# Six weight groups beside the attention instead of seven, conversions in three stages, and work on x spread out

## The chip, the cores and the metric

The kernel runs on one core of a Trainium2 chip. The metric is device time in microseconds (us) of one execution; times of several executions are given as a median. The core has a matrix engine (TensorE; PE in the profile, PEld for its weight loads), VectorE (DVE), ScalarE (ACT), GpSimd (POOL) and SyncE (SP), which here issues every DMA. Each engine takes its own instructions in order: an instruction that waits for a semaphore holds up what is queued behind it on that engine.

## The reference

```python
# q, k, v: 8 x 12 heads x 448 x 64, float32
scores = q @ k.T / sqrt(64) - log(448)
attn_out = sigmoid(scores) @ v
x = attn_out as 3584 tokens x 768
# w_gate, w_val: 768 x 1536; w_out: 1536 x 768; float64
y = (sigmoid(x @ w_gate) * (x @ w_val)) @ w_out
```

q, k and w_gate are scaled by factors, so values are large; the weights arrive as float64 and are converted on the chip.

## The kernel before

**Stages.** First comes the attention: 24 blocks `m`, of seven beats `g` each (168 beats). A beat issues the score matmuls of one piece (L465), its sigmoid on ScalarE (L473), and the value matmuls of the piece two beats back (L490). Twice a block the two halves of a finished output are added: ScalarE copies one from PSUM (L500), VectorE adds the other (L507), and x goes to DRAM. The two PSUM accumulators of a half are used again some four beats later.

Then come the first two layers in eight visits, numbered 0 to 7. Tokens are taken in four pairs of batch entries; a visit takes one pair and one of two parts of the feed-forward width: visits 0 to 3 have the first part and 56 products each (visit 0 has 53, as visits overlap a little), visits 4 to 6 have 28, visit 7 has 31. A product is nine matmuls of 128x128 by 128x448 (L620); a "tick" is one product. Seven products in place of eight make one two-by-two block product (Strassen's scheme in Winograd's form), so the operands are sums and differences of quarters of x and of quarters of a weight block; n counts the seven. Every operand is a pair of float16 tensors, high part and rest. Two units of seven products are woven into each other two ticks apart, so a product that goes on in the accumulator of another comes four ticks after it, and what reads or copies that accumulator in between (ScalarE's copy at L636, VectorE's add at L603) has three products of time. The output layer (C visits) follows with 21 x 18 matmuls for each pair.

**Conversion of weights.** A weight group is one (jp, t): two 128-column blocks of w_gate (t = 0) or w_val (t = 1), or two 128-row blocks of w_out; twelve groups of the first kind (numbered 0 to 11), six of the second. A group is four tiles of 128x384 float64. For a tile, `Words.first` makes the magnitude (L202 on VectorE in the attention, L205 on ScalarE later), clamps it on GpSimd (L186) and starts the mantissa on VectorE (L187); `Words.second` is four VectorE operations (L196 to L199), the first of which needs the clamp. `convert` is a generator; each `next` is a step. A tile takes two steps, so a group eight; then come the scale (row maxima or sums of absolutes, their broadcast by a small matmul, powers of two) and the seven operands: three quarters cast as they are, four sums made by GpSimd (L247) and cast in the same step; a step later VectorE makes the rest (L217), a step later SyncE stores. Casts are on GpSimd in the attention (L346), on ScalarE later (L343). `todo` holds work for later steps, `now` counts them.

**What sets the order.** The order is written out by hand. In the attention, `FIRST` = 7 groups are spread over `BESIDE` = 160 beats, 72 steps. In the first layers, `due` says how many steps each tick takes: 23 steps (group 7) in ticks 2 to 30 of visit 0, and 91 steps in 188 "calm" ticks: ticks 2 to 29 of visits 1 and 2, ticks from 2 on of visits 3 to 6. Group 7 belongs to the first part, so visit 0 itself needs it, from its product 46 on.

**Work on x.** For the next pair, `load_x` loads twelve tiles and takes their sums, then makes the scale while nine GpSimd subtractions run (L313), one at each `next`; `split_x` then casts 21 operands (L343, or L346 for the first pair) and makes their rests (L349) one step later. For the first pair this goes on beside blocks 7 to 23 of the attention (loads four a block, splits two a block from block 13 on); for the other pairs beside visits 0, 1 and 2 (loads from tick 2, subtractions one a tick, splits one a tick from tick 30 on).

`load_operands` keeps a ring of eight weight operands ahead of TensorE; SyncE issues these loads, the stores and all other DMAs in one order. The lines that the change touches are 168 to 199 (`Words`), 207 to 298 (`convert`), 315 to 340 (`load_x`), 546 to 569 (the attention's beats), 764 to 797 (`Visit`) and 954 to 962 (`due`).

Of the kernel before, what the change touches and what calls it, by code (L numbers as in the profile page):

```python
# [9 lines left out]
F32 = mybir.dt.float32  # L10
F16 = mybir.dt.float16
BF16 = mybir.dt.bfloat16
U32 = mybir.dt.uint32
# [7 lines left out]
P = 128  # L21
# [8 lines left out]

BESIDE = 160

AHEAD, AHEAD_FF = 4, 2

FIRST = 7

LAG = 2

# [15 lines left out]
def sigmoid_attention_glu_kernel(ctx: ExitStack, tc: tile.TileContext, qk, v, wg, wv, wo, out):  # L54
# [111 lines left out]
    class Words:  # L166


        def __init__(self, pool, sources, ahead, held, magnitude):
            self.held, self.magnitude = held, magnitude  # L170
            self.pool, self.sources, self.loaded, self.begun = pool, list(sources), [], None
            self.ahead = ahead
            for _ in range(ahead):
                self.load()
# [4 lines left out]
                nc.sync.dma_start(out=raw, in_=self.sources.pop(0))  # L179
                self.loaded.append(raw.bitcast(U32).rearrange("p (n t) -> p n t", t=2))  # L180

        def first(self, f):
            raw = self.loaded.pop(0)
            m = self.pool.tile([P, CW], U32, tag="wm", name="wm", bufs=2)
            self.magnitude(f, raw[:, :, 1])
            nc.gpsimd.tensor_scalar(out=f, in0=f, scalar1=F32_MAX, scalar2=F64_ZERO, op0=ALU.min, op1=ALU.max)  # L186
            nc.vector.tensor_scalar(out=m, in0=raw[:, :, 1], scalar1=11, scalar2=0x80000000, op0=ALU.logical_shift_left, op1=ALU.bitwise_or)  # L187
            if self.begun:
                self.load()
            self.begun = raw, f, m  # L190

        def second(self):

            raw, f, m = self.begun
            e = f.bitcast(U32)
            nc.vector.tensor_scalar(out=e, in0=e, scalar1=3, scalar2=0x3F800000, op0=ALU.logical_shift_left, op1=ALU.bitwise_and)  # L196
            nc.vector.scalar_tensor_tensor(out=e, in0=raw[:, :, 1], scalar=0xC0000000, in1=e, op0=ALU.bitwise_and, op1=ALU.bitwise_or)  # L197
            nc.vector.scalar_tensor_tensor(out=m, in0=raw[:, :, 0], scalar=21, in1=m, op0=ALU.logical_shift_right, op1=ALU.bitwise_or)  # L198
            nc.vector.scalar_tensor_tensor(out=f, in0=m, scalar=2.0 ** -31, in1=f, op0=ALU.mult, op1=ALU.mult)  # L199

    def magnitude_vector(to, bits):
# [5 lines left out]
    def convert(words, parts, ks, largest_of, cast, lag, drain_after):  # L207
# [32 lines left out]
        def operands(fs, sc, to):  # L240
            a11, a12, a21, a22 = fs
            for x, n in ((a22, 6), (a11, 0), (a12, 4)):
                yield lambda x=x, n=n: high(x, sc, to(n))
            s2 = pool.tile([P, CW], F32, tag="wf4", name="wf", bufs=2)

            def summed(n, x, y, z, op):
                nc.gpsimd.tensor_tensor(out=x, in0=y, in1=z, op=op)  # L247
# [23 lines left out]

        groups = [(w_scales[jp, t], lambda n, jp=jp, t=t: to_a(jp, t, n), True) for jp, t in parts]
        groups += [(o_scales[k], lambda n, k=k: to_op(k, n), False) for k in ks]
        for at, (sc, to, everywhere) in enumerate(groups):
            if at == drain_after:
                yield from drain()
            fs = []
            for i in range(4):
                f = pool.tile([P, CW], F32, tag=f"wf{i}", name="wf", bufs=3)
                fs.append(f)  # L280
                step(lambda f=f: words.first(f))
                yield

                def second(i=i, f=f):
                    words.second()
                    unsummed.append((f, sc.sums[:, i:i + 1]))

                step(second)
                yield
            scale = sc.steps() if everywhere else [sc.row_powers]  # L290
            for i, f in enumerate(scale):
                todo.setdefault(now + 1 + i, []).append(f)
            for i, f in enumerate(operands(fs, sc, to)):
                todo.setdefault(now + len(scale) + (0 if everywhere else 1) + i, []).append(f)
        yield from drain()

# [18 lines left out]
    def load_x(pr, new, largest_of=sum_abs):  # L315

        sc, todo = x_scales[pr], []
        for i, k in [(i, k) for i in (0, 1, 3, 2) for k in range(KC)]:
            b = 2 * pr + i % 2
            xs[i, k] = new()  # L320
            nc.sync.dma_start(out=xs[i, k], in_=x_dram[i // 2 * KC + k][:, b * S:(b + 1) * S])
            todo.append(lambda x=xs[i, k], n=len(todo): largest_of(x, sc.sums[:, n:n + 1]))
            if len(todo) > LAG:
                todo[len(todo) - 1 - LAG]()
            yield
        todo = todo[-LAG:] + sc.steps()

        def subtracted(*args):
            subtract(nc.gpsimd, *args)
            if todo:  # L330
                todo.pop(0)()

        for k in range(KC):
            xs[4, k], xs[5, k] = new(), new()
            subtracted(xs[4, k], xs[1, k], xs[0, k])
            yield
            subtracted(xs[5, k], xs[3, k], xs[4, k])
            yield
            subtracted(xs[1, k], xs[3, k], xs[1, k])
            yield  # L340

    def scaled(to, x, s):
# [1 line left out]

    def scaled_gpsimd(to, x, s):
        nc.gpsimd.tensor_scalar(out=to, in0=x, scalar1=s, scalar2=None, op0=ALU.mult)  # L346
# [94 lines left out]
    with tc.manual_schedule(), tc.tile_pool(name="att", bufs=2) as att, tc.tile_pool(name="sc", bufs=2, space=PSUM) as scp, \  # L441
# [104 lines left out]
        x_loads = load_x(0, new_x, max_abs)  # L546
        splits = split_x(0, scaled_gpsimd)
# [27 lines left out]
        for _ in weights:  # L575
            done += 1
        assert done == n_weights, (done, n_weights)
        for _ in splits:
            pass

# [180 lines left out]
    class Visit:  # L761


        def __init__(self, v_):
            (_, self.pr, part), nxt = visits[v_], visits[v_ + 1]
            self.v_, self.jps, self.b, self.keep = v_, JPS_OF_PARTS[part], dict(new_bs), nxt[0] == "C"
            self.p, self.ticks = 0, starts[v_ + 1] - starts[v_]
            self.x_loads = self.splits = self.moves = iter(())
            self.early = []
            if nxt[2] == 0:  # L770
                self.x_loads, self.splits = load_x(nxt[1], new_raw), split_x(nxt[1])
            elif not self.keep and nxt[1] != self.pr:
                self.moves = load_b(nxt[1])
            if self.keep:
                self.early = OutScale(self.pr, 1).steps()
                chain[0] = Operands([p2 for kind, p2, _ in visits if kind == "C"])

        def tick(self):
# [14 lines left out]
            beside(self.v_, p)  # L793

        def end(self):
            for _ in itertools.chain(self.x_loads, self.splits, self.moves):
                pass

        def begin(self, jp, t):
# [151 lines left out]

    new_resident[0] = make_resident

    words = Words(conv, chunks(halves_of_jps[FIRST:], range(KH)), AHEAD_FF, 4, magnitude_scalar)
    weights = convert(words, halves_of_jps[FIRST:], range(KH), sum_abs, scaled, 1, 1)
    n_one = convert_steps(1, True, 1)
    n_all = 8 * (2 * JPS - FIRST - 1) + convert_steps(KH, False, 1)
# [56 lines left out]
```

## Time and profile before

| what | value |
|---|---|
| three runs, median | 1144.42 us (1143.84 to 1144.88) |
| profiled execution | 1143.65 us |
| span of its instructions | 1141.8 us |
| granted TensorE clock, mean | 0.997 |
| attention | 4.9 to 268.4 us |
| visits 0 to 7 begin at | 268.4, 358.7, 454.2, 556.1, 654.0, 701.6, 749.3, 797.0 us |
| output layer | 851.6 us to the end |

The profile is of one execution. A row of a group of instructions gives line, engine, operation, tiles written and read, shapes and count, then busy us and mean ns of one, then the engine's idle time before them and what ended it. A row of a wait gives the engine and the waiting instruction, who released it, total us, times and longest. A row of the order of time gives start, duration, engine, line, operation and, in brackets, idle time ahead of it. A row of a stretch gives busy time (and count) of each engine in it, the granted TensorE clock as a share of full speed, the share of the DMA engines and GB/s. Durations of matmuls overlap one another; busy time of an engine is the union.

### The profile page before, as it was taken

How to read it: one execution, taken by the hardware profiler on the slowest of the kernel's cores; microseconds unless marked ns; L12 is line 12 of the kernel's file. 1: busy time of each engine (PE TensorE's matmuls, PEld its weight loads, DVE VectorE, ACT ScalarE, POOL GpSimd, SP SyncE). 2: the span in 40 equal slices, each digit the busy share in tenths (PEclk: the TensorE clock that was granted, in tenths of full speed). 3: DMA queues.
4: the chain of work that ended last, by engine and by line, in shares of the span. 5: the costliest groups of instructions: out<-in, count | busy, mean ns of one | idle time of the engine just before them, and what ended most of it. 6: DMA issues, size and time to landing. Idle time of an engine off the chain costs nothing.

```text
span 1141.8 us, 20650 instructions
## 1 busy us (share of the span) xinstructions
PE 1124.3 (98%) x7269; PEld 549.3 (48%) x7269; DVE 773.8 (68%) x1318; ACT 663.7 (58%) x1254; POOL 498.2 (44%) x435
## 2 busy tenths in 40 slices
PE   9999999999999999989999999999999999999998
PEld 3444334444555555544555455555545555555554
DVE  4588999653565675687668776763257777686773
ACT  6777667775865766757556766664355334253340
POOL 0165888970441331253123333322175285482940
PEclk9999999999999999999999999999999999999999
DMA  8699878887877756844466799967656776867644
GB/s 281 227 288 349 281 240 268 271 293 244 285 254 255 247 168 226 277 143 144 130 219 202 220 325 278 331 182 234 204 160 204 239 235 205 271 206 244 197 124 145
DMA packets 174248, 265.30 MB, mean 232 GB/s; under 512 B 49216, under 2 KB 150976, under 8 KB 174144
## 3 DMA queue, kind: packets, MB, share of 16 engines
q1 hardware_dynamic: 174144, 263.98, 72.4%
q8 instruction: 57, 0.93, 0.3%
q14 instruction: 47, 0.39, 0.1%
HBM read 182.48 MB, written 81.43 MB: 231 GB/s over the span
## 4 chain that ended last, share of the span: by engine, by line
PE 83%; DVE 6%; issue 3%; POOL 3%; ACT 2%; DMA 2%; SPq 0%; POOLq 0%; DVEq 0%; ACTq 0%
PE un L620 67%; PE av L490 8%; PE sc L465 8%; DVE whl L217 1%; POOL wf L247 1%; DVE wf L197 1%; DVE wf L196 1%; DVE wm L198 1%; POOL whl L346 1%; DVE c L603 1%; DMA p<-xd 1%; POOL wf L186 1%; DMA xd<-x 0%; ACT whl L343 0%; DMA c<-xd 0%
## 5 line engine op out<-in xcount | busy, mean ns | idle before, releaser
L620 PEld LDWEIGHTS <-A 128*128 128x128 f16 x3024 | 294.9, 98 | 278.2 <-issue 2.6
L620 PE MATMUL un<-b,v 128*128 128x448 f16 x1512 | 298.1, 354 | 6.4 <-ACT c L636 4.9
L620 PE MATMUL un<-b,A 128*128 128x448 f16 x1512 | 296.6, 353 | 1.6 <-DVE c L603 1.6
L620 PE MATMUL un<-hh,A 128*128 128x448 f16 x1008 | 273.1, 353 | 0.0
L620 PEld LDWEIGHTS <-v 128*128 128x128 f16 x1512 | 148.0, 98 | 146.4 <-issue 9.7
L473 ACT ACTIVATE a<-sc,bias 128x896 f32<-128x896 f32 x168 | 169.1, 1007 | 74.9 <-PE sc L465 65.5
L620 PE MATMUL un<-hl,A 128*128 128x448 f16 x504 | 177.7, 353 | 0.0
L490 PE MATMUL av<-a,v 64*64 64x448 f32 x1344 | 167.1, 540 | 3.7 <-DVE x L507 3.6
L465 PE MATMUL sc<-qk 64*64 64x448 f32 x1344 | 167.1, 541 | 0.4 <-ACT a L473 0.4
L186 POOL TENSOR_SCALAR wf<-wf 128x384 f32<-128x384 f32 x72 | 40.0, 555 | 267.5 <-ACT wf L205 167.0
L827 POOL TENSOR_TENSOR g<-c,g 128x448 f32<-128x448 f32 x44 | 56.6, 1288 | 164.6 <-DVE c L603 99.9
L465 PEld LDWEIGHTS sc<-qk 64*64 64x64 f32 x1344 | 55.2, 135 | 77.8 <-issue 65.7
L490 PEld LDWEIGHTS av<-a,v 64*64 64x64 f32 x1344 | 54.2, 134 | 76.4 <-issue 68.8
L812 ACT ACTIVATE g<-c,back 128x448 f32<-128x448 f32 x72 | 47.9, 665 | 67.3 <-DVE c L603 63.7
L603 DVE TENSOR_TENSOR c<-un,u 128x448 f32<-128x448 f32 x72 | 44.7, 621 | 62.4 <-PE un L620 59.9
L313 POOL TENSOR_TENSOR b<-b 128x448 f32<-128x448 f32 x48 | 67.5, 1442 | 40.6 <-DVE hl L349 40.6
L313 POOL TENSOR_TENSOR v<-v 128x448 f32<-128x448 f32 x48 | 64.0, 1361 | 33.2 <-DVE hl L349 29.2
L247 POOL TENSOR_TENSOR wf<-wf 128x384 f32<-128x384 f32 x72 | 75.7, 1057 | 3.8 <-DVE whl L217 3.8
L507 DVE TENSOR_TENSOR x<-av,x 128x448 f32<-128x448 f32 x48 | 29.7, 619 | 46.2 <-ACT x L500 45.1
L313 POOL TENSOR_TENSOR r<-r 128x448 f32<-128x448 f32 x36 | 44.0, 1231 | 33.1 <-DVE b L349 32.6
L197 DVE SCALAR_TENSOR_TENSOR wf<-wraw,wf 128x384 uint32<-128x384 uint32 x72 | 54.9, 763 | 2.5
L636 ACT COPY p<-un 128x448 f32<-128x448 f32 x48 | 25.3, 526 | 50.5 <-PE un L620 50.5
(344 smaller groups left out, 1350.0 us busy)
## 6 DMA issues: line engine op xcount, KB each, us to landing
A<-ad SPq DMA_DIRECT2D x168, 192.0 KB, 3.4
A<-oo SPq DMA_DIRECT2D x168, 192.0 KB, 2.8
qk<-qk SPq DMA_DIRECT2D x23, 896.0 KB, 5.4
h<-g SPq DMA_DIRECT2D x88, 224.0 KB, 3.5
ad<-whl SPq DMA_DIRECT2D x84, 192.0 KB, 4.3
bd<-b SPq DMA_DIRECT2D x30, 448.0 KB, 3.8
b<-bd SPq DMA_DIRECT2D x30, 448.0 KB, 5.9
v<-vv SPq DMA_DIRECT2D x24, 448.0 KB, 4.8
```

Source lines behind the costliest of these rows:

```text
L186: nc.gpsimd.tensor_scalar(out=f, in0=f, scalar1=F32_MAX, scalar2=F64_ZERO, op0=ALU.min, op1=ALU.max)
L197: nc.vector.scalar_tensor_tensor(out=e, in0=raw[:, :, 1], scalar=0xC0000000, in1=e, op0=ALU.bitwise_and, op1=ALU.bitwise_or)
L247: nc.gpsimd.tensor_tensor(out=x, in0=y, in1=z, op=op)
L313: engine.tensor_tensor(out=to, in0=x, in1=y, op=ALU.subtract)
L465: nc.tensor.matmul(sc[halves[u], h, :S], lhsT=qkt[halves[h], p, k0:k0 + HP], rhs=qkt[halves[h], p, :S], start=True, stop=True)
L473: nc.scalar.activation(a, sc[:, :, :S], AF.Sigmoid, bias=bias, scale=scale)
L490: nc.tensor.matmul(avs[key][halves[h], :S], lhsT=vt[halves[u], g, h], rhs=a[halves[u], h], start=start, stop=g == last)
L507: nc.vector.tensor_tensor(out=x, in0=other, in1=x, op=ALU.add)
L603: engine.tensor_tensor(out=to, in0=x, in1=y, op=ALU.add)
L620: nc.tensor.matmul(acc, lhsT=w, rhs=m, start=begin and i == 0, stop=i == len(terms) - 1, skip_group_check=not begin)
L812: nc.scalar.activation(gates[i], acc, AF.Sigmoid, scale=of_unit[0])
L827: nc.gpsimd.tensor_tensor(out=h, in0=acc, in1=gates[i], op=ALU.mult)
```

## The change

1. `FIRST` is 6: six groups (67 steps) in the same 160 beats. Groups 6 and 7 are converted in visit 0, 34 steps in ticks 2 to 33.
2. A tile's conversion has stages: the magnitude of the next tile is issued in the step that begins the current tile; its clamp in the step after; its VectorE work in the two steps after that (two operations, then three). A sum's cast moves to the step after the sum. The buffers of `wm` and of the sum `wf4` become one each, the raw tiles of the first layers three; the next raw tile is loaded at the end of a tile's work.
3. The other 94 steps are spread evenly over the 250 ticks from tick 2 of visit 1 to the end of visit 6, so also over the ticks of visits 1 and 2 in which x is split.
4. Subtractions of x are a generator of their own: beside the attention two a block from block 11 on, in visits 0 to 2 every second tick from tick 17 on. The scale's steps follow the loads, one at each `next`. Loads in the attention are three a block, splits five in two blocks from block 14 on; in the visits splits start at tick 29.
5. Of the first pair's casts the first, third and so on run on ScalarE, the others on GpSimd.

The diff, cut to its core:

```diff
-AHEAD, AHEAD_FF = 4, 2
+AHEAD, AHEAD_FF = 4, 3
-FIRST = 7
+FIRST = 6
...
-        def first(self, f):
+        def begin(self, f):
             raw = self.loaded.pop(0)
-            m = self.pool.tile([P, CW], U32, tag="wm", name="wm", bufs=2)
             self.magnitude(f, raw[:, :, 1])
+            self.begun.append((raw, f))
+
+        def limit(self):
+            raw, f = self.begun[-1]
             nc.gpsimd.tensor_scalar(out=f, in0=f, scalar1=F32_MAX, scalar2=F64_ZERO, op0=ALU.min, op1=ALU.max)
-            nc.vector.tensor_scalar(out=m, in0=raw[:, :, 1], scalar1=11, scalar2=0x80000000, op0=ALU.logical_shift_left, op1=ALU.bitwise_or)
-            if self.begun:
-                self.load()
-            self.begun = raw, f, m
-        def second(self):
-            raw, f, m = self.begun
+        def first(self):
+            raw, f = self.begun[0]
             e = f.bitcast(U32)
             nc.vector.tensor_scalar(out=e, in0=e, scalar1=3, scalar2=0x3F800000, op0=ALU.logical_shift_left, op1=ALU.bitwise_and)
             nc.vector.scalar_tensor_tensor(out=e, in0=raw[:, :, 1], scalar=0xC0000000, in1=e, op0=ALU.bitwise_and, op1=ALU.bitwise_or)
+        def second(self):
+            raw, f = self.begun.pop(0)
+            m = self.pool.tile([P, CW], U32, tag="wm", name="wm", bufs=1)
+            nc.vector.tensor_scalar(out=m, in0=raw[:, :, 1], scalar1=11, scalar2=0x80000000, op0=ALU.logical_shift_left, op1=ALU.bitwise_or)
             nc.vector.scalar_tensor_tensor(out=m, in0=raw[:, :, 0], scalar=21, in1=m, op0=ALU.logical_shift_right, op1=ALU.bitwise_or)
+            self.load()
             nc.vector.scalar_tensor_tensor(out=f, in0=m, scalar=2.0 ** -31, in1=f, op0=ALU.mult, op1=ALU.mult)
...
-            s2 = pool.tile([P, CW], F32, tag="wf4", name="wf", bufs=2)
+            s2 = pool.tile([P, CW], F32, tag="wf4", name="wf", bufs=1)
             def summed(n, x, y, z, op):
                 nc.gpsimd.tensor_tensor(out=x, in0=y, in1=z, op=op)
-                high(x, sc, to(n))
+                todo.setdefault(now + 1, []).append(lambda: high(x, sc, to(n)))
...
+                def first():
+                    if next_[1] or next_[0] != drain_after:
+                        begun.append(value(*next_))
+                    words.first()
+                def second():
+                    if any(begun):
+                        words.limit()
                     words.second()
                     unsummed.append((f, sc.sums[:, i:i + 1]))
...
-        todo = todo[-LAG:] + sc.steps()
-        def subtracted(*args):
-            subtract(nc.gpsimd, *args)
-            if todo:
-                todo.pop(0)()
+        for f in todo[-LAG:] + sc.steps():
+            f()
+            yield
+    def subtract_x(new):
         for k in range(KC):
...
+    casts = itertools.cycle((scaled, scaled_gpsimd))
+    def scaled_in_turn(*args):
+        next(casts)(*args)
...
-                if m >= first_x and g in (1, 3, 4, 6):
+                if m >= first_x and g in (1, 3, 5):
                     next(x_loads, None)
-                if m >= first_x + 6 and g in (2, 5):
+                if m >= first_x + 4 and g in (2, 6):
+                    next(x_sums, None)
+                if m >= first_x + 7 and (g in (2, 5) or g == 0 and m % 2):
                     next(splits, None)
...
+            if p >= 17 and p % 2:
+                next(self.x_sums, None)
-            if p >= 30:
+            if p >= 29:
                 next(self.splits, None)
...
-    calm = [t for v_ in range(1, n_a - 1) for t in range(starts[v_] + 2, starts[v_] + 30 if v_ < 3 else starts[v_ + 1])]
+    calm = range(starts[1] + 2, starts[n_a - 1])
-    for ticks, n in ((range(2, 31), n_one), (calm, n_all)):
+    for ticks, n in ((range(2, 34), n_first), (calm, n_all)):
```

More of the change, by code (lines that the diff above doesn't have):

```diff
@@ L273, in convert, with value @@
         groups += [(o_scales[k], lambda n, k=k: to_op(k, n), False) for k in ks]
+        def value(at, i):
+            if at < len(groups) and i < 4:
+                value_of[at, i] = pool.tile([P, CW], F32, tag=f"wf{i}", name="wf", bufs=3)
+                words.begin(value_of[at, i])
+                return True
+        value_of = {}
         for at, (sc, to, everywhere) in enumerate(groups):
@@ L276, in convert @@
                 yield from drain()
-            fs = []
-            for i in range(4):
[L279 to L284, printed above, removed]
+            if at in (0, drain_after):
+                step(lambda: value(at, 0))
+                yield
+                step(words.limit)
+                yield
+            for i in range(4):
+                f = value_of[at, i]
+                next_ = (at, i + 1) if i < 3 else (at + 1, 0)
+                begun = []
+                def first():
[5 more added lines that the diff above has]
+                        words.limit()
                     words.second()
                     unsummed.append((f, sc.sums[:, i:i + 1]))
+                step(first)
+                yield
                 step(second)
                 yield
+            fs = [value_of.pop((at, i)) for i in range(4)]
             scale = sc.steps() if everywhere else [sc.row_powers]
@@ L325, in load_x @@
             yield
-        todo = todo[-LAG:] + sc.steps()
-        def subtracted(*args):
-            subtract(nc.gpsimd, *args)
-            if todo:
-                todo.pop(0)()
+        for f in todo[-LAG:] + sc.steps():
+            f()
+            yield
+    def subtract_x(new):
         for k in range(KC):
             xs[4, k], xs[5, k] = new(), new()
-            subtracted(xs[4, k], xs[1, k], xs[0, k])
+            subtract(nc.gpsimd, xs[4, k], xs[1, k], xs[0, k])
             yield
-            subtracted(xs[5, k], xs[3, k], xs[4, k])
+            subtract(nc.gpsimd, xs[5, k], xs[3, k], xs[4, k])
             yield
-            subtracted(xs[1, k], xs[3, k], xs[1, k])
+            subtract(nc.gpsimd, xs[1, k], xs[3, k], xs[1, k])
             yield
@@ L544, in new_x @@
             return sb(tag) if tag in SUMS else att.tile([P, S], F32, tag=tag, name="xt", bufs=1)
-        x_loads = load_x(0, new_x, max_abs)
-        splits = split_x(0, scaled_gpsimd)
+        x_loads, x_sums = load_x(0, new_x, max_abs), subtract_x(new_x)
+        splits = split_x(0, scaled_in_turn)
         beat = 0
@@ L577, in sigmoid_attention_glu_kernel @@
         assert done == n_weights, (done, n_weights)
+        assert next(x_loads, None) is None and next(x_sums, None) is None
         for _ in splits:
@@ L767, in __init__ @@
             self.p, self.ticks = 0, starts[v_ + 1] - starts[v_]
-            self.x_loads = self.splits = self.moves = iter(())
+            self.x_loads = self.x_sums = self.splits = self.moves = iter(())
             self.early = []
             if nxt[2] == 0:
-                self.x_loads, self.splits = load_x(nxt[1], new_raw), split_x(nxt[1])
+                self.x_loads, self.x_sums, self.splits = load_x(nxt[1], new_raw), subtract_x(new_raw), split_x(nxt[1])
             elif not self.keep and nxt[1] != self.pr:
@@ L795, in end @@
         def end(self):
-            for _ in itertools.chain(self.x_loads, self.splits, self.moves):
+            for _ in itertools.chain(self.x_loads, self.x_sums, self.splits, self.moves):
                 pass
@@ L952, in sigmoid_attention_glu_kernel @@
     new_resident[0] = make_resident
+    in_first = 2 * len(JPS_OF_PARTS[0]) - FIRST
     words = Words(conv, chunks(halves_of_jps[FIRST:], range(KH)), AHEAD_FF, 4, magnitude_scalar)
-    weights = convert(words, halves_of_jps[FIRST:], range(KH), sum_abs, scaled, 1, 1)
-    n_one = convert_steps(1, True, 1)
-    n_all = 8 * (2 * JPS - FIRST - 1) + convert_steps(KH, False, 1)
-    calm = [t for v_ in range(1, n_a - 1) for t in range(starts[v_] + 2, starts[v_] + 30 if v_ < 3 else starts[v_ + 1])]
+    weights = convert(words, halves_of_jps[FIRST:], range(KH), sum_abs, scaled, 1, in_first)
+    n_first = convert_steps(in_first, True, 1)
+    n_all = 8 * (2 * JPS - FIRST - in_first) + convert_steps(KH, False, 1)
+    calm = range(starts[1] + 2, starts[n_a - 1])
     due = {}
-    for ticks, n in ((range(2, 31), n_one), (calm, n_all)):
+    for ticks, n in ((range(2, 34), n_first), (calm, n_all)):
         for i, t in enumerate(ticks):
```

4 lines of the change are left out of this document (2 added, 2 removed).

## The prediction

> **What bounds the kernel now.** I read the page first: whether TensorE is the bound, and what stops it.
>
> ```profile
> span 1141.8 us, 20650 instructions
> PE 1124.3 (98%) x7269; PEld 549.3 (48%) x7269; DVE 773.8 (68%) x1318; ACT 663.7 (58%) x1254; POOL 498.2 (44%) x435
> ```
>
> TensorE is busy for 98%, and the diff takes no matmul of the products away. So the most that it can win is the time in which TensorE stands still or runs slowly, and I looked for that place by place: the attention in three stretches (4.87 is its first matmul, 268.37 its end), then visits 0 to 3 from their first to their last product. The columns are the stretch, then busy us and count for PE, PEld, DVE, ACT, POOL, then the granted clock, DMA share, GB/s.
>
> ```profile
> 4.87:120.00 115.13, 114.74 (x1215) 46.10 (x1214) 84.30 (x185) 85.12 (x99) 44.42 (x44) 1.00 0.87 295
> 120.00:150.00 30.00, 26.34 (x248) 9.77 (x244) 29.05 (x56) 17.12 (x23) 25.73 (x24) 0.94 0.67 216
> 150.00:268.37 118.37, 118.37 (x1255) 48.16 (x1247) 83.45 (x142) 87.89 (x103) 89.97 (x72) 1.00 0.82 271
> ...
> 268.37:358.73 90.36, 90.36 (x484) 46.69 (x481) 52.05 (x94) 61.40 (x139) 28.51 (x26) 1.00 0.81 271
> 358.73:454.18 95.45, 95.45 (x508) 49.35 (x507) 58.44 (x94) 61.73 (x146) 27.77 (x27) 1.00 0.68 221
> 454.18:556.09 101.91, 97.61 (x507) 49.83 (x506) 73.11 (x121) 67.96 (x160) 34.87 (x33) 0.98 0.53 172
> 556.09:653.97 97.88, 95.77 (x507) 49.33 (x506) 73.81 (x147) 60.30 (x143) 32.22 (x34) 1.00 0.67 206
> ```
>
> Attention: 118.37 us for 1255 matmuls is 0.0943 us each; the 248 of 120 to 150 would take 23.4 us at that rate and take 30. I count 6.0 of these 6.6 us as lost, as the broadcasts of scales lie closer there. Visits 1, 2 and 3 have the same 56 products: 95.45 us is the undisturbed price (1.704 a product), so visit 2 loses 6.46 us and visit 3 2.43. Together 14.9 us, part of it at a reduced clock (0.94, 0.98). Visit 0 (53 products, 90.36 us) loses nothing.
>
> What TensorE waits for there, and then who holds that up:
>
> ```profile
> PE un L620 <- ACT c L636: 4.9, 3, 2.8
> PE av L490 <- DVE x L507: 3.6, 2, 2.7
> ...
> POOL wf L186 <- ACT wf L205: 167.0, 30, 25.2
> POOL wf L186 <- DVE wf L202: 81.1, 24, 8.3
> ACT whl L343 <- POOL wf L247: 50.9, 29, 4.8
> ```
>
> Neither the ScalarE copy nor the VectorE add is late of itself. In visit 3 the order of time shows the chain:
>
> ```profile
> 626.87 0.54 ACT L205 ACTIVATE wf<-wraw 128x384 f32<-128x384 f32 x1
> 627.49 0.51 POOL L186 TENSOR_SCALAR wf<-wf 128x384 f32<-128x384 f32 x1 [6.27 <-ACT wf L205]
> 627.96 1.95 POOL L247 TENSOR_TENSOR wf<-wf 128x384 f32<-128x384 f32 x2
> 629.00 0.62 ACT L343 ACTIVATE whl<-wf,w51s 128x384 f16<-128x384 f32 x1 [1.59 <-POOL wf L247]
> 629.64 0.68 DVE L217 SCALAR_TENSOR_TENSOR whl<-wf,w51s,whl 128x384 f16<-128x384 f32 x1 [3.15 <-ACT whl L343]
> 631.28 0.51 ACT L636 COPY c<-un 128x448 f32<-128x448 f32 x1
> 631.84 2.43 PE L620 MATMUL un<-b,v 128*128 128x448 f16 x12 [1.86 <-ACT c L636]
> ```
>
> GpSimd's clamp waits for the magnitude of the same tile, issued just ahead of it; the sum behind it starts late; ScalarE, whose queue holds the cast of that sum, stands 1.59 us; VectorE 3.15 us; and the copy that TensorE needs comes at 631.28. Queues in order make a ring out of work that is nowhere urgent. In the attention it is VectorE and GpSimd, both nearly full (29.05 and 25.73 of 30 us).
>
> **The change, part by part.** The profiled execution took 1143.65 us, 0.77 under the median of the three runs (1144.42); I sum against 1143.65 and add 0.77.
>
> *Magnitude a step ahead, clamp a step later, cast a step after its sum.* No instruction more or less, but each step's partner on another engine was issued at least a step before. At the new rate of 94 steps in 250 ticks (0.376) a step is 4.5 us, longer than any wait in the chain above. So visit 3, whose only added load is this work, should lose nothing: -2.4. Visit 2 had subtractions of x at one a tick beside it; now one every second tick: -6.5.
>
> *Attention.*
>
> ```profile
> L247 POOL TENSOR_TENSOR wf<-wf 128x384 f32<-128x384 f32 x28 | 29.6, 1056 | 0.0
> L186 POOL TENSOR_SCALAR wf<-wf 128x384 f32<-128x384 f32 x28 | 15.5, 553 | 83.3 <-DVE wf L202 81.1 <-DMA v<-vv 2.1
> L346 POOL TENSOR_SCALAR whl<-wf,w11s 128x384 f16<-128x384 f32 x7 | 10.2, 1459 | 0.9 <-DVE invw L121 0.5
> L346 POOL TENSOR_SCALAR b<-xt,x0s 128x448 f16<-128x448 f32 x9 | 14.4, 1601 | 0.0
> L313 POOL TENSOR_TENSOR xt<-g,xt 128x448 f32<-128x448 f32 x4 | 4.6, 1162 | 0.1
> ```
>
> A group costs GpSimd 4 x 1.056 + 4 x 0.553 + 7 x 1.459 = 16.6 us. Before, one came per 17.8 beats (8 of 72 steps in 160 beats), 26.9 us at 16 matmuls or 1.51 us a beat: 62%. The nine subtractions of x (1.16 each) fell into 16 beats, 24 us: 43% more, 105% in all, which is the stall at 120 to 150. After, a group comes per 19.1 beats, 28.8 us (58%), and the subtractions take 4.5 blocks of seven beats, 48 us: 22%, together 80%. Casts of x: eleven of 21 leave GpSimd (11 x 1.6 = 18 us); ScalarE does them at the 0.66 us of the row on `b<-r` below, 7 us beside 87.89 of 118 us busy. VectorE's share falls by a seventh of its conversions. I expect 0.5 us of the 6.0 to stay: -5.5. Bounds: -6.0, and 0 if VectorE alone was the limit.
>
> *The group that moves, and the tails.* Visit 0 now takes 34 steps in 32 ticks instead of 23 in 29, and visits 1 and 2 convert also from tick 30 on, beside the splitting of x, where nothing was converted. The first row below is such a tail in visit 1, the others are visits with conversions and no work on x:
>
> ```profile
> 409.90:450.80 40.90, 40.90 (x218) 21.12 (x217) 28.58 (x45) 29.16 (x62) 10.53 (x9) 1.00 0.72 243
> 654.00:701.60 47.60, 47.60 (x253) 24.58 (x252) 33.71 (x66) 29.19 (x68) 15.68 (x17) 1.00 1.02 327
> 701.60:749.30 47.70, 47.70 (x254) 24.60 (x252) 35.17 (x70) 31.99 (x76) 14.87 (x17) 1.00 0.86 264
> ...
> 271.80:302.40 30.60, 30.60 (x164) 15.86 (x163) 15.69 (x32) 21.19 (x56) 8.26 (x10) 1.00 0.94 315
> ...
> L603 DVE TENSOR_TENSOR c<-un,u 128x448 f32<-128x448 f32 x72 | 44.7, 621 | 62.4 <-PE un L620 59.9
> ...
> L825 DVE SCALAR_TENSOR_TENSOR g<-un,back,g 128x448 f32<-128x448 f32 x22 | 14.9, 679 | 13.8 <-PE un L620 8.4 <-ACT junk L102 4.2 <-ACT u L636 1.1
> ...
> L205 ACT ACTIVATE wf<-wraw 128x384 f32<-128x384 f32 x44 | 23.7, 539 | 2.4 <-DMA wraw<-wv 1.4 <-DMA wraw<-wo 0.9
> L102 ACT ACTIVATE junk<-wf 128x384 bf16<-128x384 f32 x44 | 22.9, 521 | 12.4 <-DVE wf L199 8.4 <-DVE w50m L124 1.4 <-DVE o3m L124 1.3
> L343 ACT ACTIVATE whl<-wf,w50s 128x384 f16<-128x384 f32 x7 | 4.3, 609 | 8.1 <-POOL wf L247 8.1
> L343 ACT ACTIVATE b<-r,x3s 128x448 f16<-128x448 f32 x21 | 13.8, 660 | 0.0
> ```
>
> A visit of 28 ticks has 12 adds (0.62) and 4 products (taken as 0.7) of its own, 10.3 us. So the 56 ticks of the two rows spent 68.9 - 20.6 = 48.3 us of VectorE on 27 steps (0.484 a tick): 1.78 a step. A tail of 24 ticks gets 9 steps, 16 us, on 28.58 us less some 1.8 of leftover conversion: 42.8 of 40.9 us, 105%. TensorE bears a delay: a product that goes on in an accumulator comes four ticks after its predecessor, so the add or copy between has three products, 5.1 us. An excess of 1.9 us fits into that, with some 3 us for waits. ScalarE gets 9 steps of some 1.1 us (in eight steps four magnitudes of 0.54, four sums of 0.52 and seven casts of 0.61, and the reading out of four sums): 39 of 40.9. In visit 0 four more tiles come into 271.8 to 302.4: 8 steps x 1.78 = 14 us at most on 15.69 of 30.6, which is 98%, and ScalarE 21.19 + 5. I take +1 for each tail and +0.3 for visit 0: +2.3. Bounds: 0 (all in the slack), and the lock below.
>
> *At nothing.* The weight load moves behind the operation that empties its buffer:
>
> ```profile
> SPq L179 <- DVE wm L198: 67.3, 35, 7.6
> ```
>
> The DMA queue stands behind VectorE there already; operands of the products queue behind it, eight buffers (13.6 us) ahead, and the attention's next q and k seven beats (10.5 us) ahead. This costs only if VectorE is late by more than about 5 us. The third raw buffer is paid by the single `wm` and `wf4`. The group moved out of the attention is due at product 39, its last store at tick 25. The visits from 4 on have 0.376 instead of 0.484 steps a tick, and lose nothing now.
>
> **Sum:** -5.5 - 2.4 - 6.5 + 2.3 = -12.1; 1143.65 - 12.1 + 0.77 = 1132.3 us.
>
> **The rivals.**
>
> *VectorE is locked by GpSimd in the tails (slower).* The same operation alone and beside GpSimd's subtractions:
>
> ```profile
> 482.56 0.56 DVE L197 SCALAR_TENSOR_TENSOR wf<-wraw,wf 128x384 uint32<-128x384 uint32 x1
> 499.94 1.38 DVE L197 SCALAR_TENSOR_TENSOR wf<-wraw,wf 128x384 uint32<-128x384 uint32 x1
> ...
> 497.15 5.16 POOL L313 TENSOR_TENSOR r<-r 128x448 f32<-128x448 f32 x4
> ```
>
> A tail holds about 30 such operations (22 of tiles, 8 splits), 0.82 us more each: 24.6 us if all are hit. VectorE's 42.8 then grow by 24.6 f, against 46.0 that the slack bears; f counts hits beyond those already in the 1.78. From f = 0.43 the two tails cost the 14.4 us won elsewhere; at 0.6 they cost 23, and the time is 1153. For it: 490 to 516 was such a stretch. Against it: GpSimd would be busy 10.53 + 9 x 0.8 = 17.8 of 40.9 us (44%), only little over the 33% of the two rows that gave 1.78, and the subtractions end near tick 33. Chance 0.10. The Trainium skill, SBUF — State Buffer, section "SBUF: two separate sides", calls this an exclusive lock, in which the loser waits for the whole instruction. By that rule in full, 42.8 + 17.8 = 60.6 us would need 14.6 us in each tail, an estimate of 1159; the trace bears it out for single operations (0.56 against 1.38), not for the sum, as 29.05 and 25.73 us fit into 30.
>
> *The tails fill, without the lock.* Waits among three engines at 95 to 105% use up the slack: 4 us in each tail and 2 in visit 0 instead of 2.3 in all: 1140. For it: visit 2 stalled with VectorE at 73 of 102 us. Against: tail and conversions each ran without a stall. Chance 0.17.
>
> *The ring still closes.* ScalarE's sum of absolutes of a tile still waits for VectorE and stands ahead of the next magnitude; half of the 14.9 us stays: -7.4 + 2.3, or 1139.3. Chance 0.13.
>
> **How the numbers follow.** The forecast has 0.60. A measurement of this kernel tells 0.2% (2.3 us) from no change. Faster by more: 0.60 + 0.13 + 0.13 of the 0.17 = 0.86; within: 0.04; slower: 0.10. Range: 1129.0 (all 14.9 us, 1129.5, and half a us between runs) to 1140.5, which takes in the third rival and half of the second and leaves out about 0.18.
>
> **What would show it.** Right: 120 to 150 with the clock at 1.00 and the matmuls of the other stretches; visits 2 and 3 at 95 to 97 us; no wait of the clamp on the magnitude; ScalarE's wait for L247's sums gone; VectorE over 95% in ticks 30 to 53 of visits 1 and 2 with under 2 us lost. Wrong: visits 1 and 2 over 99 us, conversions there at 1.2 us and more, or TensorE still waiting for the attention's add.

## The result and the profile after

The changed kernel takes 1149.27 us (median of six runs, 1148.4 to 1150.75) against 1143.23 us (six runs) of the kernel before: a ratio of 1.0054, 95% interval 1.0041 to 1.0068. It is slower, by half a per cent; 1132.3 us had been forecast, with 1140.5 as the upper end of its range. The profiled execution has a span of 1148.9 us, 7.1 more than before.

The page's head, then the attention from 120 us to its end, then visits 0 to 3 from product to product (columns as before):

```profile
span 1148.9 us, 20691 instructions
PE 1126.9 (98%) x7268; PEld 550.3 (48%) x7268; DVE 785.0 (68%) x1310; ACT 677.0 (59%) x1284; POOL 485.6 (42%) x417
```

```profile
120.00:150.00 30.00, 28.97 (x300) 11.61 (x296) 29.41 (x53) 21.27 (x27) 22.75 (x20) 1.00 0.83 290
150.00:262.98 112.98, 112.98 (x1204) 45.52 (x1193) 69.93 (x127) 89.01 (x109) 68.42 (x54) 1.00 0.79 266
...
262.98:360.40 97.42, 92.42 (x484) 47.23 (x481) 74.40 (x127) 68.86 (x159) 38.26 (x34) 0.98 0.86 288
360.40:455.86 95.46, 95.46 (x508) 49.40 (x507) 64.85 (x113) 63.88 (x153) 31.90 (x31) 1.00 0.64 215
455.86:565.74 109.88, 100.94 (x510) 50.71 (x508) 92.67 (x156) 76.92 (x185) 46.88 (x42) 0.95 0.59 194
565.74:661.08 95.34, 95.34 (x506) 49.29 (x504) 70.23 (x126) 58.30 (x134) 30.57 (x31) 1.00 0.69 201
```

The attention ends at 262.98 instead of 268.37 (-5.4); visit 0 takes 97.42 instead of 90.36 (+7.1), visit 1 the same, visit 2 109.88 instead of 101.91 (+8.0), visit 3 95.34 instead of 97.88 (-2.5). These four sum to +7.1, the whole difference of the spans. VectorE is busy for 92.67 us in visit 2, where it was 73.11, and for 74.40 in visit 0, where it was 52.05.

What TensorE waits for now, with the old wait of GpSimd's clamp (total us, times, longest):

```profile
POOL wf L189 <- ACT wf L211: 154.4, 23, 37.1
...
PE un L653 <- ACT u L669: 7.1, 2, 4.5
PE un L621 <- DVE each L114: 4.2, 2, 3.8
```

The wait at L621 is new. L621 is the small matmul that broadcasts a weight group's row maxima; it stands in TensorE's own queue, at a place fixed by hand three steps after the maxima. Visit 0's stretch in VectorE's and TensorE's order of time, after the row of the stretch:

```profile
283.00:309.00 26.00, 21.00 (x109) 10.47 (x107) 24.57 (x45) 17.93 (x51) 15.84 (x15) 0.97 0.85 274
...
302.49 1.38 DVE L205 SCALAR_TENSOR_TENSOR wf<-wm,wf 128x384 f32<-128x384 uint32 x1
303.79 1.34 DVE L223 SCALAR_TENSOR_TENSOR whl<-wf,w30s,whl 128x384 f16<-128x384 f32 x1
306.50 0.97 DVE L114 TENSOR_SCALAR each<-w31m 128x128 bf16<-128x128 f32 x1
...
307.53 0.23 PE L621 MATMUL un<-ident,each 128*128 128x128 bf16 x1 [3.78 <-DVE each L114]
```

VectorE works for 24.57 of 26 us without catching up; it comes to the operation on the second group's maxima that the broadcast needs (L114) at 306.5, and all products behind the broadcast have waited 3.78 us. Of visit 0's 7.06 us this stand is the largest part. After it two products take 5.14 us instead of 3.41, at a granted clock of 0.54 to 0.50 (307.5 to 311). And 1.22 us were lost before it, at 301.88, to a load of `h`: SyncE issued it behind a weight load that had waited for VectorE's L203. In visit 2's tail the way is another one:

```profile
411.30:452.30 41.00, 41.00 (x220) 21.22 (x218) 37.60 (x62) 29.52 (x67) 15.31 (x13) 1.00 0.69 240
...
506.80:565.70 58.90, 50.42 (x241) 24.70 (x240) 53.07 (x92) 40.25 (x90) 22.07 (x19) 0.91 0.49 160
```

```profile
516.98 0.54 ACT L211 ACTIVATE wf<-wraw 128x384 f32<-128x384 f32 x1
522.34 0.62 ACT L368 ACTIVATE whl<-wf,w50s 128x384 f16<-128x384 f32 x1 [4.82 <-DVE w50s L120]
...
525.25 0.51 ACT L669 COPY u<-un 128x448 f32<-128x448 f32 x1
...
525.81 3.29 PE L653 MATMUL un<-b,v 128*128 128x448 f16 x9 [2.59 <-ACT u L669]
528.89 5.57 PE L653 MATMUL un<-b,A 128*128 128x448 f16 x27
```

The first row is visit 1's tail (VectorE 92%, nothing lost), the second visit 2's. There ScalarE stands 4.82 us at a cast, until VectorE has finished that group's scale, then has 2.9 us of other work to do before the copy at 525.25 that TensorE needs. And after the stand nine matmuls take 3.08 us to the next product's start instead of 1.70: the clock is 0.54 in these 3.1 us and 0.91 over the stretch.

### The profile page after: what moved, and what is told of

Read it like the earlier page. It is cut to its first block, busy times and chain, and to the rows that moved or that the text cites. A ratio compares the mean times of both kernels' runs of the same rounds, so it can differ in the third digit from the quotient of the medians.

```text
span 1148.9 us, 20691 instructions
## 1 busy us (share of the span) xinstructions
PE 1126.9 (98%) x7268; PEld 550.3 (48%) x7268; DVE 785.0 (68%) x1310; ACT 677.0 (59%) x1284; POOL 485.6 (42%) x417
## 4 chain that ended last, share of the span: by engine, by line
PE 83%; DVE 8%; DMA 3%; issue 2%; ACT 2%; POOL 1%; SPq 0%; DVEq 0%; POOLq 0%; ACTq 0%
PE un L653 65%; PE sc L495 9%; PE av L520 9%; DVE whl L223 1%; DVE wm L203 1%; DMA r<-xd 1%; DVE c L636 1%; DVE wm L202 1%; DMA u<-xd 1%; DVE b L379 1%; DMA A<-ad 1%; DMA ad<-whl 1%; DVE wf L205 1%; DMA c<-xd 0%; ACT junk L102 0%
## 5 line engine op out<-in xcount | busy, mean ns | idle before, releaser
L653 PE MATMUL un<-b,A 128*128 128x448 f16 x1512 | 300.0, 355 | 1.6 <-DVE c L636 1.6
L520 PE MATMUL av<-a,v 64*64 64x448 f32 x1344 | 159.3, 538 | 1.0 <-DVE x L537 1.0
L495 PE MATMUL sc<-qk 64*64 64x448 f32 x1344 | 160.1, 541 | 0.0
L189 POOL TENSOR_SCALAR wf<-wf 128x384 f32<-128x384 f32 x72 | 44.8, 622 | 222.0 <-ACT wf L211 154.4
L495 PEld LDWEIGHTS sc<-qk 64*64 64x64 f32 x1344 | 52.6, 134 | 76.7 <-issue 62.0
L253 POOL TENSOR_TENSOR wf<-wf 128x384 f32<-128x384 f32 x72 | 83.9, 1169 | 8.1 <-DVE whl L223 7.3
L520 PEld LDWEIGHTS av<-a,v 64*64 64x64 f32 x1344 | 51.7, 133 | 73.6 <-issue 70.4
L339 POOL TENSOR_TENSOR r<-r 128x448 f32<-128x448 f32 x36 | 46.6, 1300 | 28.3 <-DVE b L379 25.3
L102 ACT ACTIVATE junk<-g 128x448 bf16<-128x448 f32 x88 | 50.6, 574 | 12.7 <-POOL g L862 8.9
```

Of the source, the lines that this page charges most:

```text
L102: nc.scalar.activation(junk[:, :x.shape[-1]], x, AF.Abs, accum_out=to)
L339: engine.tensor_tensor(out=to, in0=x, in1=y, op=ALU.subtract)
L495: nc.tensor.matmul(sc[halves[u], h, :S], lhsT=qkt[halves[h], p, k0:k0 + HP], rhs=qkt[halves[h], p, :S], start=True, stop=True)
L520: nc.tensor.matmul(avs[key][halves[h], :S], lhsT=vt[halves[u], g, h], rhs=a[halves[u], h], start=start, stop=g == last)
L653: nc.tensor.matmul(acc, lhsT=w, rhs=m, start=begin and i == 0, stop=i == len(terms) - 1, skip_group_check=not begin)
```

## The experiments

Theory after the first look ("load"): VectorE has more work than time where the change puts conversions: two groups in visit 0's first ticks, and the tail of visit 2 beside the splitting of x. Rivals: the staging costs by itself (the clamp now runs beside the tile's VectorE operations and locks them, the deferred casts make new waits), or the broadcast's fixed place does.

**One part undone at a time.** `seven_groups`:

```diff
-FIRST = 6
+FIRST = 7
```

> The changed kernel with seven groups beside the attention, so only one in visit 0 (26 steps in the same 32 ticks); all else as changed. If two groups overfill VectorE in visit 0 (load): visit 0 back from 97.4 to 90 to 91 us, visit 2 still about 110, the attention 0 to 4 us longer than 263.0, in all 1143 to 1147. If the staging itself (the clamp beside the tile's VectorE operations, or the deferred casts) is what costs: visit 0 keeps half of its loss, 94 us or more, in all about 1148.

`calm_tails`:

```diff
-    calm = range(starts[1] + 2, starts[n_a - 1])
+    calm = [t for v_ in range(1, n_a - 1) for t in range(starts[v_] + 2, starts[v_] + 30 if v_ < 3 else starts[v_ + 1])]
```

> The changed kernel with no conversions in ticks 30 and later of visits 1 and 2, as before the change: the 94 steps lie in the 188 calm ticks, 0.5 a tick instead of 0.376. If conversions beside the splitting of x cost visit 2 its time (load): visit 2 from 109.9 to 96 to 98 us, visits 1 and 3 at 95 to 97, visit 0 still 97.4, in all 1135 to 1139. If the staging costs: visit 2 at 104 or more, visit 3 above 97, in all 1144 or more.

`old_places` has both edits.

> Both of these: seven groups, and conversions in the ticks of before; what is left of the change is the staging, the spaced work on x and the casts on ScalarE. Load: visits 0 to 3 at 90.4, 95.5, 96 to 98, 95.4, the attention 263 to 267, in all 1128 to 1133. Staging: at most half of the 14.9 us that the kernel before lost is won, 1137 or more.

`even_rate_alone` is the kernel before with the line of `calm` alone exchanged the other way round.

> The kernel before with one thing of the change: its 91 steps spread over the 250 ticks, also beside the splitting of x in visits 1 and 2; no staging. Load: visit 2 at 106 or more instead of 101.9, visit 3 at 95.4 to 96, in all 1144 to 1150. Staging as the cause: visit 2 no longer than 102, in all 1138 to 1142.

Measured (ratio to the kernel before, with its interval; places from the profiles, us). The ratios are to runs of the kernel before taken beside each set, with medians of 1143.23 us for the changed kernel, 1142.77 for the other four here, and 1142.13 and 1142.57 for later ones:

| kernel | median | ratio | attention ends | visit 0 | visit 1 | visit 2 | visit 3 |
|---|---|---|---|---|---|---|---|
| before | 1142.77 | | 268.37 | 90.36 | 95.45 | 101.91 | 97.88 |
| changed | 1149.27 | 1.0054 [1.0041, 1.0068] | 262.98 | 97.42 | 95.46 | 109.88 | 95.34 |
| seven_groups | 1147.54 | 1.0038 [1.0023, 1.0053] | 267.19 | 90.35 | 95.45 | 109.78 | 95.34 |
| calm_tails | 1140.14 | 0.9980 [0.9971, 0.9989] | 262.52 | 97.29 | 95.40 | 98.09 | 95.45 |
| old_places | 1139.55 | 0.9969 [0.9956, 0.9982] | 267.37 | 90.36 | 95.39 | 98.10 | 95.45 |
| even_rate_alone | 1146.48 | 1.0033 [1.0023, 1.0044] | 268.59 | 90.70 | 95.93 | 106.80 | 96.71 |

The row of visit 0 in `seven_groups`, of visit 2 in `calm_tails`, and of visit 2 in `even_rate_alone`:

```profile
267.19:357.54 90.35, 90.35 (x483) 46.79 (x480) 53.74 (x93) 62.16 (x139) 28.96 (x26) 1.00 0.83 277
```

```profile
455.21:553.30 98.09, 95.84 (x509) 49.40 (x508) 72.60 (x120) 67.46 (x159) 36.04 (x32) 1.00 0.55 177
```

```profile
455.22:562.02 106.80, 98.10 (x509) 49.84 (x508) 83.30 (x147) 74.00 (x177) 42.91 (x41) 0.98 0.62 202
```

The losses come and go with the places, each by itself: one group less in visit 0 takes its 7 us away, leaves visit 2 as it was and lets the attention end 4.2 us later; the tails without conversions take 11.8 us from visit 2; and the even rate costs visit 2 4.9 us without any staging. With the same ticks as before, the staging and the spaced work on x win: visit 2 98.1 for 101.9, visit 3 95.45 for 97.88. Visit 3 has no work on x, so there it is the staging; in visit 2 no run tells the two apart. `seven_groups` and `calm_tails` were expected at up to 1147 and 1139 and lie slightly above. `old_places` was expected at 1128 to 1133 and is at 1139.55: its attention ends at 267.37, 4.4 us later than with six groups, visit 2 keeps 2.6 us over the 95.45 of a free visit, and visits 4 and 5 take 49.42 and 48.32 us for 47.67; that 0.5 steps a tick is a little too much there is likely, but not tested.

**The rivals, and a try at a better place.** `no_clamp` leaves out L189:

```diff
-            nc.gpsimd.tensor_scalar(out=f, in0=f, scalar1=F32_MAX, scalar2=F64_ZERO, op0=ALU.min, op1=ALU.max)
+            pass
```

> The changed kernel with GpSimd's clamp of the magnitudes left out (72 instructions). If it is the lock between GpSimd and VectorE at the tile's operations that overfills visits 0 and 2: L203's mean from 0.73 to about 0.58, and at least half of visit 0's 7 us and of visit 2's 14.4 us is gone (94 and 103 or less). If it is the amount of VectorE work: the tile's five operations fall by under 0.3 us of 3.37, visit 0 at 95 to 97, visit 2 at 106 or more.

VectorE's tile operations, in the changed kernel and then without the clamp (last numbers before the bar's end: mean ns):

```profile
L203 DVE SCALAR_TENSOR_TENSOR wm<-wraw,wm 128x384 uint32<-128x384 uint32 x48 | 35.2, 733 | 1.6
L205 DVE SCALAR_TENSOR_TENSOR wf<-wm,wf 128x384 f32<-128x384 uint32 x48 | 34.2, 713 | 1.7
L196 DVE SCALAR_TENSOR_TENSOR wf<-wraw,wf 128x384 uint32<-128x384 uint32 x48 | 32.3, 673 | 1.6
L202 DVE TENSOR_SCALAR wm<-wraw 128x384 uint32<-128x384 uint32 x48 | 32.3, 672 | 0.0
L195 DVE TENSOR_SCALAR wf<-wf 128x384 uint32<-128x384 uint32 x48 | 27.7, 576 | 1.4 <-POOL wf L189 1.4
```

```profile
L203 DVE SCALAR_TENSOR_TENSOR wm<-wraw,wm 128x384 uint32<-128x384 uint32 x48 | 38.6, 804 | 1.6
L196 DVE SCALAR_TENSOR_TENSOR wf<-wraw,wf 128x384 uint32<-128x384 uint32 x48 | 34.1, 711 | 1.6
L205 DVE SCALAR_TENSOR_TENSOR wf<-wm,wf 128x384 f32<-128x384 uint32 x48 | 34.0, 708 | 1.7
L195 DVE TENSOR_SCALAR wf<-wf 128x384 uint32<-128x384 uint32 x48 | 28.5, 594 | 0.8 <-ACT wf L211 0.8
L202 DVE TENSOR_SCALAR wm<-wraw 128x384 uint32<-128x384 uint32 x48 | 26.1, 544 | 0.0
```

The five means sum to 3.37 and 3.36 us over all visits, so on the whole the clamp does not lengthen VectorE's work. In visit 2 it does: there the five means sum to 3.64 and 3.30 us, and the same 156 instructions keep VectorE busy for 92.67 and 88.26 us. Visit 2 falls to 106.27, 3.6 us less (1145.26 us, one run), and visit 0 stays at 96.68. Single profiles differ somewhat: visit 2 is 108.64 in `casts_on_gpsimd` below, which changes nothing there. `cast_after_scale` puts every operand a step after its scale:

```diff
-                todo.setdefault(now + len(scale) + (0 if everywhere else 1) + i, []).append(f)
+                todo.setdefault(now + len(scale) + 1 + i, []).append(f)
...
-        return 8 * n_groups + lag + (TAIL + 4 if everywhere else TAIL)
+        return 8 * n_groups + lag + (TAIL + 5 if everywhere else TAIL)
```

> The changed kernel with every operand of a weight group one step later, so that no cast on ScalarE stands in the step in which VectorE finishes the scale. If that same-step wait (4.8 us of ScalarE at 522) is the way into TensorE's stall: visit 2 falls from 109.9 to 105 or less. If VectorE is simply overfull: ScalarE is held up at the next wait for VectorE instead (the gates), visit 2 at 107 or more.

Visit 2 is at 106.79 (1144.38 us, one run), between the two that were expected: the wait at the cast is worth some 3 us, and most of the 14.4 us that visit 2 loses stays. `casts_on_gpsimd` puts all casts of x's first pair on GpSimd:

```diff
-    casts = itertools.cycle((scaled, scaled_gpsimd))
+    casts = itertools.cycle((scaled_gpsimd,))
```

> The changed kernel with all casts of x for the first pair on GpSimd again. If the attention's gain comes from fewer groups and spaced subtractions: it still ends at 262.5 to 263.5. If ScalarE's casts are what frees GpSimd: it ends at 264.5 or later. Visits as in the changed kernel.

It ends the attention at 261.96 (1149.72 us, one run), so the casts on ScalarE show no part in its gain.

`late_broadcast` makes the broadcast, and with it the end of the scale and the operands, a step later:

```diff
-            scale = sc.steps() if everywhere else [sc.row_powers]
+            scale = [sc.rows, idle, idle, idle, sc.spread, idle, sc.finish] if everywhere else [sc.row_powers]
...
-        return 8 * n_groups + lag + (TAIL + 4 if everywhere else TAIL)
+        return 8 * n_groups + lag + (TAIL + 5 if everywhere else TAIL)
...
-    for ticks, n in ((range(2, 34), n_first), (calm, n_all)):
+    for ticks, n in ((range(2, 35), n_first), (calm, n_all)):
```

> The changed kernel with the broadcast of a weight group's scale on TensorE one step later after its row maxima (and the operands with it), at the same rate in visit 0. If the stand at the broadcast is a cost of its own: visit 0 from 97.4 to 93 or less. If it only shows that VectorE is late: the loss moves to a copy or an add, visit 0 at 95 or more.

Visit 0 is at 96.83 (1143.96 us, one run). TensorE's waits from 255 to 360 us there:

```profile
PE un L653 <- ACT u L669: 3.2, 1, 3.2
PE un L621 <- DVE each L114: 1.3, 1, 1.3
```

The stand at the broadcast falls from 3.8 to 1.3 us and turns up at a copy. `stretched_first` spreads visit 0's steps over 39 ticks and keeps conversions out of visit 2's tail alone:

```diff
-    calm = range(starts[1] + 2, starts[n_a - 1])
+    calm = [t for v_ in range(1, n_a - 1) for t in range(starts[v_] + 2, starts[v_] + 30 if v_ == 2 else starts[v_ + 1])]
-    for ticks, n in ((range(2, 34), n_first), (calm, n_all)):
+    for ticks, n in ((range(2, 41), n_first), (calm, n_all)):
```

> The changed kernel with its two groups in visit 0 spread over 39 ticks instead of 32 (0.87 steps a tick instead of 1.06), and no conversions in the tail of visit 2 alone (ticks 30 on); visit 1's tail keeps them. Load: attention ends near 263, visit 0 at 90.4 to 93, visits 1, 2, 3 at 95.5, 98, 95.4, in all 1130 to 1135. If what matters in visit 0 is the fixed distance from the row maxima to the broadcast on TensorE and not the rate: visit 0 stays at 95 or more, in all 1137 or more.

It is at 1143.29 us, ratio 1.0005 [0.9997, 1.0014]: visits 0 and 1 are 95.82 and 103.85.

```profile
262.41:358.23 95.82, 91.55 (x484) 46.66 (x481) 74.93 (x127) 68.33 (x159) 38.19 (x34) 1.00 0.87 289
358.23:462.08 103.85, 98.25 (x508) 50.13 (x507) 71.34 (x128) 68.22 (x166) 35.85 (x35) 0.97 0.66 221
...
409.30:462.08 52.78, 47.18 (x238) 23.66 (x236) 44.72 (x74) 35.92 (x83) 19.53 (x18) 0.94 0.70 244
```

The expectation by load failed twice, and by its numbers the other one, the fixed distance to the broadcast, was met in visit 0. But TensorE waits there for ScalarE's copies (1.7 us), a load of a weight operand (1.6) and VectorE's add (0.9), and not at L621. A lower rate carries the same work (74.93 us against 74.40) into the ticks in which x is split; and visit 1's tail, free in the changed kernel, loses 8.4 us with 0.44 steps a tick: there the conversions have come further by tick 30, from tiles alone to tiles and rests of operands. The last row is that tail: VectorE has 44.72 us of work for 26 products, which need 44.3.

**The dose.** `no_sign`, `three_of_five` and `none_of_five` leave out one (L196), two (L195 and L196) and all five of a tile's VectorE operations (also L202, L203 and L205):

```diff
-            nc.vector.tensor_scalar(out=e, in0=e, scalar1=3, scalar2=0x3F800000, op0=ALU.logical_shift_left, op1=ALU.bitwise_and)
-            nc.vector.scalar_tensor_tensor(out=e, in0=raw[:, :, 1], scalar=0xC0000000, in1=e, op0=ALU.bitwise_and, op1=ALU.bitwise_or)
```

`no_sign` lacks the second line, `three_of_five` both.

> The changed kernel without the operation on VectorE that puts the sign in (L196; 72 of 0.67 us; so the weights lose their signs). Nothing else is taken away. If VectorE's load is the cause: a fifth of each tile's VectorE time gone, visit 0 at 92 to 94 instead of 97.4, visit 2 at 98 to 103 instead of 109.9. If waits among the engines are: both within 2 us of the changed kernel.

> The changed kernel without two of a tile's five VectorE operations (L195 and L196, 1.25 of 3.37 us; the weights come out wrong in exponent and sign); casts, sums, clamps, broadcasts and stores are all there. If VectorE's amount is the cause, one for one: some 5.5 tiles in visit 2's tail, 6.9 us less, visit 2 at 102 to 104; visit 0 at 91 to 93. If the waits from engine to engine cost by themselves: visit 2 at 106 or more, as without the sign alone (107.0).

> The changed kernel without all five VectorE operations of a tile (3.37 us; the weights are left as magnitudes); casts, sums, clamps, rests, broadcasts and stores stay. If VectorE's amount is the cause: visit 0 at 90.4 to 91, visit 2 at 95.5 to 98. If the waits from engine to engine cost by themselves: visit 2 at 101 or more.

Visit 2 of the three in this order, and visit 0 of the last:

```profile
449.45:556.42 106.97, 99.15 (x509) 50.18 (x508) 82.86 (x144) 75.34 (x182) 45.07 (x41) 0.97 0.59 195
```

```profile
449.23:552.45 103.22, 96.38 (x510) 49.43 (x509) 76.91 (x129) 72.31 (x175) 43.83 (x40) 1.00 0.60 195
```

```profile
260.15:350.56 90.41, 90.41 (x484) 46.86 (x481) 52.06 (x87) 68.60 (x159) 35.82 (x34) 1.00 0.89 310
...
446.02:541.58 95.56, 95.56 (x510) 49.53 (x508) 55.04 (x98) 75.20 (x181) 42.09 (x40) 1.00 0.68 216
```

Visit 2 goes 109.88, 106.97, 103.22, 95.56 and visit 0 97.42, 93.78, 92.80, 90.41 as VectorE's work falls from 92.7 to 82.9, 76.9 and 55.0 us in the one and from 74.4 to 68.6, 65.5 and 52.1 in the other. With none of it nothing is lost in visits 0 to 3, though ScalarE's and GpSimd's instructions and the broadcasts are all there (spans 1139.6, 1135.7, 1124.8 us). `no_sign` was expected at 98 to 103 us in visit 2 and is at 106.97: 9.8 us less of VectorE's time bought only 2.9 us, and why is not shown. So the time that VectorE spends on the tiles is shown as the cause; the waits only set where TensorE stands. How much of that time is the operations themselves and how much is blocking by GpSimd these runs do not separate, since an operation that is left out takes both with it.

**A version that beats both.** `six_late` has six groups, the calm ticks of before, operands a step after the scale and the broadcast a step later:

```diff
-            scale = sc.steps() if everywhere else [sc.row_powers]
+            scale = [sc.rows, idle, idle, idle, sc.spread, sc.finish] if everywhere else [sc.row_powers]
...
-                todo.setdefault(now + len(scale) + (0 if everywhere else 1) + i, []).append(f)
+                todo.setdefault(now + len(scale) + 1 + i, []).append(f)
...
-        return 8 * n_groups + lag + (TAIL + 4 if everywhere else TAIL)
+        return 8 * n_groups + lag + (TAIL + 5 if everywhere else TAIL)
...
-    for ticks, n in ((range(2, 34), n_first), (calm, n_all)):
+    for ticks, n in ((range(2, 35), n_first), (calm, n_all)):
```

`seven_late` is `old_places` with the second and third of these edits.

> Six groups, conversions in the calm ticks of before, operands one step after the scale, and the broadcast on TensorE one step later after the row maxima. If visit 0's loss is TensorE standing at the broadcast: visit 0 at 93 or less, in all 1132 to 1135. If VectorE is overfull there whatever waits first: visit 0 at 95 to 97, in all 1136 to 1139.

> Seven groups, conversions in the ticks of before, the staging and the spaced work on x of the change, and every operand of a weight group one step after its scale. The attention should lose 1 to 1.5 us less than with the operands in the scale's own step (it ended at 267.4), visit 0 at 90.4, visit 2 at 97 to 98: 1136 to 1139, if the waits in the scale's step cost there too; 1139 to 1141 if not.

`six_late` is at 1135.58 us, ratio 0.9940 [0.9926, 0.9954]: attention to 260.99, visits 95.88, 95.40, 97.02, 95.45. `seven_late` is at 1138.40, 0.9960 [0.9946, 0.9974]; its attention ended later (269.59), not earlier, perhaps as the additional step falls into the same 160 beats, which is not tested. Visit 0 of `six_late` still loses 5.5 us, with VectorE at 72.87 us, as was expected if VectorE is overfull there whatever waits first:

```profile
260.99:356.87 95.88, 91.40 (x484) 46.66 (x481) 72.87 (x127) 68.44 (x159) 37.47 (x34) 1.00 0.88 292
```

## Why the prediction was wrong

**Right.** The attention's -5.5 (measured -5.4) and visit 3's -2.4 (-2.5). The first was partly luck. The working put the stall at 120 to 150 down to GpSimd at 105% and its end mainly to the spaced subtractions. With these and seven groups (`old_places`) the stall at 120 to 150 is gone, but the loss comes up again behind it:

```profile
120.00:150.00 30.00, 30.00 (x324) 11.95 (x316) 29.34 (x58) 22.42 (x28) 22.87 (x21) 1.00 0.90 290
150.00:180.00 30.00, 29.52 (x306) 11.74 (x300) 29.38 (x58) 22.43 (x28) 25.09 (x21) 1.00 0.84 283
180.00:210.00 30.00, 27.81 (x280) 10.87 (x278) 25.45 (x46) 20.83 (x26) 24.27 (x20) 1.00 0.72 235
```

The changed kernel has 326 matmuls in each of the last two stretches. TensorE's waits in this attention are for VectorE's add (2.7 us in four waits), and VectorE is busy for 29.38 of the 30 us from 150 on. With seven groups the attention ends at 267.19 (`seven_groups`), so 4.2 us come from the group that left and 1.2 from all the rest, and the casts on ScalarE give nothing.

Of the signs that were named, the clock at 1.00 in 120 to 150 came, the full rate there did not (300 matmuls). The clamp's wait for the magnitude stayed (154.4 us for 167.0) and cost visit 3 nothing. ScalarE's wait for GpSimd's sums fell from 50.9 to 4.4 us.

**Wrong: "I take +1 for each tail and +0.3 for visit 0: +2.3."** It was +14.4 in visit 2 (against 95.45), 0 in visit 1 and +7.1 in visit 0. The place and the engine were named; four things in the step failed. (The -6.5 of visit 2 was too much as well: without conversions in its tail visit 2 comes to 98.1, which is -3.8. What keeps the other 2.65 us is not shown.)

1. *The price of a step.* 1.78 us was a mean over visits 4 and 5, where a tile's five operations took 2.81 us. In the stretch from 506.8 to 565.7 VectorE worked for 53.07 us. The 26.5 products of it need 45.2, so this is 117% instead of 105%. There a tile's five operations took 3.38 us, and the groups there also have a scale for all rows.
2. *One price for both tails.* Steps differ: visit 1's tail fell on the beginning of the row of groups, with four tiles and one rest; visit 2's had up to six tiles and ten rests. That the mean hid it, `stretched_first` showed by moving visit 1's tail on.
3. *The slack.* "TensorE bears a delay ... 5.1 us. An excess of 1.9 us fits into that". The slack has to bear VectorE's delay and ScalarE's backlog together: 4.82 us of standing at VectorE's scale and then 2.9 us of queued work. An engine that waits is late by the wait plus what queued up meanwhile. The slack did not hold at less than the 105% reckoned either: with VectorE at 101% of the products' time (44.72 of 44.3 us) visit 1 lost 8.4 us in `stretched_first`.
4. *The broadcast "at nothing".* "The group moved out of the attention is due at product 39": I looked at its stores, not at its broadcast, an instruction in TensorE's own queue that waits for VectorE. In visit 0, at 98% by my own sum, that cost 3.78 us at one stroke. Undone, the loss moved to a copy, so it was the way in and not the cause. The weight load behind VectorE, at nothing too, was a small cost: SyncE's queue stands at it for 178.4 us instead of 67.3, and TensorE's 1.22 us at the load of `h` in visit 0 followed one such stand.

To this comes the clock, which the sum left out: after stands of 2.6 and 4.5 us the next products ran at about half rate, some 4.6 of visit 2's 14.4 us (1.38 and 0.30 after the first; 1.61 and 1.27 after the second), and 1.7 of visit 0's 7.1 us after the stand of 3.78.

**The rivals.** The slower one had the side and the place, and its mechanism has a part. A tile's five operations sum to 2.38 us where the timeline shows them undisturbed, to 2.81 in the visits that gave the price, and to 3.38 in visit 2's tail. For the five and a half tiles there that is 3.1 us above the price, an estimate, of the 7.9 us by which VectorE's 53.07 exceed 45.2. In the rival's terms f is about 0.13 (3.1 of 24.6 us) and not the 0.43 from which it turns the change slower. `no_clamp` agrees that the part is real and not the whole: 3.6 of visit 2's 14.4 us. "The tails fill" had the mechanism and priced it at 4 us a tail. "The ring still closes" fell: visit 3 loses nothing.

## What to carry to other kernels

An engine with a mean of 68% can be the bound in two stretches of 26 and 59 us; sum its work for each stretch in which streams meet, by counting the instructions that fall there, and do not multiply a mean step. Near 100% slack is no answer, since other engines add their backlog to the delay: the tail of visit 1 lost nothing at 92% and 8.4 us at 101%. Before a step is moved, look for those of its instructions that stand in the bound engine's own queue.

## What the runs showed of the hardware

TensorE's clock falls after short stands: after 2.59 us of waiting nine matmuls took 3.08 us (525.81 to 528.89) instead of 1.70, at a granted clock of 0.54. In the kernel before, a stand of 2.75 us had the same effect (clock 0.50 from 146.3 to 148.6). Stands of 1.22 us (at 535.7 in the changed kernel) and 1.86 us (at 631.84 in the kernel before) had no such effect; the clock stayed at 1.00.

The Trainium skill, TensorE: Matmul & The Clock Gate, section "What's actually happening", names an idle window of about 3.4 us, so 2.6 us would not be enough; here it was.

VectorE's operations take longer beside GpSimd's: without the 72 clamps a tile's five operations in visit 2 took 3.30 us instead of 3.64.
